# Block-sparse attention feeding a soft mixture of experts: k and q of a head pair transposed into one PSUM tile and copied out at once, loads issued at other places in a pair

## The chip, the cores and the metric

The kernel runs on one core of a Trainium2 chip. The metric is the device time of one execution in microseconds, as the median of several executions. "The profiled execution" is one further execution, recorded by the hardware profiler; its span goes from its first to its last recorded instruction.

The engines are named as in the profile: PE is TensorE's matrix multiplication and PEld its weight loads, DVE is VectorE, ACT is ScalarE, POOL is GpSimd, SP is SyncE. PSUM is the memory that TensorE writes to; here it has eight banks.

## What is computed

Attention over 4 batches × 8 heads, 768 positions, 64 dimensions a head, with keys in 24 chunks of 32. Each query keeps six chunks, chosen by an upper bound of its scores; then a soft mixture of experts over the 3072 × 512 result:

```python
k_min = np.min(k_chunks, axis=3); k_max = np.max(k_chunks, axis=3)
ub = sum_d(maximum(q * k_min, q * k_max))            # one bound per query and chunk
ub = np.where(causal, ub, -1e9)
top_chunks = np.argsort(ub, axis=-1)[..., -6:]
scores = scale * q @ k.T                             # kept where selected and causal
x = softmax(scores) @ v                              # 3072 x 512 after the heads are joined

logits = x @ phi                                     # 512 x 32: 8 experts of 4 slots
slot_input = softmax(logits, over tokens).T @ x
slot_out[e] = relu(slot_input[e] @ w1[e]) @ w2[e]    # w1 512 x 1024, w2 1024 x 512
out = softmax(logits, over slots) @ slot_out         # 3072 x 512 f32
```

## The kernel before

**Tiling.** Two heads make a pair: 128 partitions hold 2 × 64 dimensions. There are 16 pairs, four to a batch. k and q arrive in bf16 with positions on the partitions, and TensorE transposes them, six column blocks of 128 positions for each of two heads. Scores are computed transposed, keys on partitions and queries in columns, and only the causal blocks, packed in six groups (`GROUPS`, L29). The prediction calls them s0 to s5 (`scores(i, g)`, L316) and their exponentials on ScalarE e0 to e5 (`expo(i, g)`, L340). Groups 0, 1 and 4 have 2 × 512 columns, groups 2, 3 and 5 have 2 × 384.

**Order.** The order of instructions on each engine is the order of the Python calls, written by hand (`tc.manual_schedule()`, L84). An engine works its list in order; a wait holds up all that stands behind it. Between engines the pools decide: a tile drawn from a pool takes the buffer of the tile drawn `bufs` earlier under the same tag, and its first writer waits for the last reader of that tile. The PSUM pools are (L88 to L90): `p_sc`, two buffers of two banks, tag "sc", for the score tiles; `p_at`, one buffer of two banks for the value product; `p_tp`, two buffers of one bank, tag "tp", for all transposes and bounds.

**One pair** `i` of the main loop (L618 to L696) works on five pairs at once. In the order of the calls:

- `scores`/`expo` groups 0 and 1 of pair i. `mask` (L353), called by `expo`, zeroes the blocks on the diagonal on GpSimd.
- `ubound(i+1)` (L272): thirteen matmuls of the split q (`qpn`) with the chunk minima and maxima (`bd`).
- `normalise(i-2)` (L380, DVE).
- `select(i+1)` (L289): twelve DVE maxima of eight, a cast on GpSimd (L296, "the selection's cast"), one comparison on DVE.
- `transposes(i+2, "k")` (L225) into a "tp" tile, `evac_T(i+2, "k")` (L237): a ScalarE copy to `kT`.
- `load(i+5)` (L147) of k and q: DMA issues from GpSimd, f32 to bf16 on the way, into a ring of five.
- `pv(i-1)` (L362), the value product, blocks 0 to 2; score groups 2 and 3; `x_transposes(i-2)` (L393); `pv` block 3.
- `transposes(i+2, "q")` and `evac_T(i+2, "q")`; `kmin` (L246), `evac_x` (L405), `kmax` (L252) on DVE.
- `load_v(i+2)` (L160) and `weights(i)` (L555): DMA issues from GpSimd. `wplan` (L552) says how many of the experts' 16 weights of 1 MB each pair issues; `load_w` (L137) issues first the eight of w1, then the eight of w2 in the order `LATE` (L79), so that the last one issued is that of expert 4.
- score groups 4 and 5; `ns_transposes(i+1)` (L302) and `evac_ns(i+1)` (L311, DVE), which bring the selection to the form in which the scores add it; `pv` blocks 4 and 5; `qsplit(i+2)` (L262, DVE).

The selection enters a score group as extra matmuls (L333) that accumulate a large negative number from `nsT`.

The pairs 3, 7 and 11 are each the last of a batch; the mixture's softmax for the batch runs three pairs later, in pairs 6, 10 and 14 (`slots`, L619; the calls `moe(...)`), its logits two pairs later, in pairs 5, 9 and 13. In the slots pairs the k and q loads stand behind score group 3. Pairs 0 to 2 are transposed in the prologue (L561 to L616).

**After the loop** (from L698): the last pair's values, the last batch's logits and softmax, `experts_in` (L824, uses w1), `experts_out` and `shared_out` (L864, L872, w2), `last_expert_out` (L888, the last weight loaded), then the product with the slots' outputs, scaled and stored in 512 KB pieces.

Of the kernel before, what the change touches and what calls it, by code (L numbers as in the profile page):

```python
# [10 lines left out]
BF16 = mybir.dt.bfloat16  # L11
# [48 lines left out]
def kernel(  # L60
# [10 lines left out]
    nc = tc.nc  # L71
# [9 lines left out]
    EARLY = 14  # L81
# [13 lines left out]
    ident = static.tile([P, P], BF16, name="ident")  # L95
# [29 lines left out]
    tp3 = i_ctx.enter_context(tc.tile_pool(name="tp3", bufs=3, side="right"))  # L125
# [11 lines left out]
    def load_w(i):  # L137

        if i < E:
            src = moe_w1[i].rearrange("(a p x) f -> p a (x f)", p=P, x=2)  # L140
            dst = w_sb[i].rearrange("p (a f) -> p a f", a=NDG // 2)
        else:
            src = moe_w2[LATE[i - E]].rearrange("(a p x) d -> p a (x d)", p=P, x=4)
            dst = w_sb[i].rearrange("p (a f) -> p a f", a=NFG // 4)
        nc.gpsimd.dma_start(out=dst, in_=src)  # L145

    def load(i, nm):  # L147

        b, j = divmod(i, NPB)
        t = ring[nm][i % 5]  # L150
        src = {"k": k, "q": q}[nm][b, 2 * j:2 * j + 2]
        nc.gpsimd.dma_start(out=t, in_=src.rearrange("h (p g) d -> p h (g d)", p=P))  # L152
        st[nm, i] = t
# [6 lines left out]
    def load_v(i):  # L160
        b, j = divmod(i, NPB)
        nc.gpsimd.dma_start(  # L162
            out=v_t[i % NV][:, :, :, :D],
            in_=v[b, 2 * j:2 * j + 2].rearrange("h (g p) d -> p h g d", p=P),
        )
# [59 lines left out]
    def transposes(i, nm):  # L225

        ps = p_tp.tile([P, NQT, P], BF16, name="tr_ps", tag="tp")
        src = st.pop((nm, i))
        for g in range(NQT):
            for h in range(2):  # L230
                nc.tensor.matmul(  # L231
                    ps[h * 64:(h + 1) * 64, g, :], lhsT=src[:, h, g * D:(g + 1) * D], rhs=ident,
                    is_transpose=True,
                )
        st[nm + "ps", i] = ps

    def evac_T(i, nm):  # L237

        t = tp3.tile([P, S], BF16, name=nm + "T", tag=nm + "T")
        nc.scalar.copy(  # L240
            t.rearrange("d (p g) -> d p g", g=NQT),
            st.pop((nm + "ps", i)).rearrange("d g p -> d p g"),
        )
        st[nm + "T", i] = t

    def kmin(i):  # L246
        kT = st["kT", i].rearrange("d (c x) -> d c x", x=CH)
# [24 lines left out]
    def ubound(i):  # L272
        ps = p_tp.tile([P, NJ, 2, 2, NCHUNK], F32, name="ub_ps", tag="tp")
        qpn, bd = st.pop(("qpn", i)), st.pop(("bd", i))
        nc.tensor.matmul(
            ps.rearrange("p j h x c -> p (j h x c)"), lhsT=qgrp.rearrange("p a b -> p (a b)"),
            rhs=caus.rearrange("p j h x c -> p (j h x c)"), start=True, stop=False,
        )
        for t in range(NQT):
            o = ps[:, t % NJ, :, t // NJ, :]  # L280
            for x in range(2):
                nc.tensor.matmul(  # L282
                    o, lhsT=qpn[:, x, t * P:(t + 1) * P],
                    rhs=bd[:, x],
                    start=False, stop=(t == NQT - 1 and x == 1),
                )
        st["ubps", i] = ps
# [28 lines left out]
    def scores(i, g):  # L316
        ps = p_sc.tile([P, 2, 512], F32, name="sc_ps", tag="sc")
        kT, qT, nsT = st["kT", i], st["qT", i], st["nsT", i]
        for kg, q0, w, c in (GROUPS_LAST if i == LAST else GROUPS)[g]:
            qs = slice(kg * P + q0, kg * P + q0 + w)  # L320
            for h in range(2):
                r = slice(h * 64, (h + 1) * 64)
                nc.tensor.matmul(  # L323
                    ps[:, h, c:c + w], lhsT=kT[r, kg * P:(kg + 1) * P], rhs=qT[r, qs],
                    start=True, stop=False,
                )
            t0, t1 = kg + q0 // P, kg + (q0 + w) // P
            runs = [(x, max(t0, x * NJ), min(t1, (x + 1) * NJ)) for x in range(2)]
            runs = [r for r in runs if r[1] < r[2]]
            for x, f, l in runs:  # L330
                for h in range(2):
                    r = slice(h * 64, (h + 1) * 64)
                    nc.tensor.matmul(  # L333
                        ps[:, h, c + (f - t0) * P:c + (l - t0) * P],
                        lhsT=smask[r, x, kg].rearrange("p a b -> p (a b)"),
                        rhs=nsT[r, (f - x * NJ) * P:(l - x * NJ) * P], start=False, stop=(l == t1),
                    )
        st["scps", i, g] = ps

    def expo(i, g, masked=True):  # L340
        pieces = (GROUPS_LAST if i == LAST else GROUPS)[g]
        w = sum(x[2] for x in pieces)
        if w == 512:
            e = ep.tile([P, 2, 512], BF16, name="e_sb", tag="e_sb")
        else:
            e = ep3.tile([P, 2, 384], BF16, name="e3_sb", tag="e3_sb")
        nc.scalar.activation(e[:, :, :w], st.pop(("scps", i, g))[:, :, :w], func=ACT.Exp, scale=scale)  # L347

        st["e", i, g] = e
        if masked:  # L350
            mask(i, g)
# [191 lines left out]
    def have(i):  # L543
        return 0 <= i < NPAIR

    def moe(step, i):

        if have(i) and i % NPB == NPB - 1:
            step(i // NPB)


    wplan = {1: 1, 3: 1, 4: 1, 5: 1, 7: 1, 8: 1, 9: 1, 10: 1, 11: 1, 12: 1, 13: 2, 14: 1, 15: 1}  # L552
    nw = 2

    def weights(i):  # L555
        nonlocal nw
        for _ in range(wplan.get(i, 0)):
            load_w(nw)
            nw += 1
# [58 lines left out]
    for i in range(1, NPAIR):  # L618
        slots = have(i - 3) and (i - 3) % NPB == NPB - 1  # L619
        if i >= EARLY:  # L620
            wt = ctx.enter_context(tc.tile_pool(name=f"wt{i}", bufs=1))
            w_sb.append(wt.tile([P, NFG * Dm], BF16, name=f"w_sb{i}"))
            weights(i)
        scores(i, 0)
        expo(i, 0)
        moe(moe_max, i - 3)
        scores(i, 1)
        expo(i, 1)
        if have(i + 1):
            ubound(i + 1)  # L630
        moe(moe_bound, i - 3)
        if have(i - 2):
            normalise(i - 2)
        if i == LAST:
            moe_ct_copy(B - 2)
        if have(i + 1):
            select(i + 1)
        moe(moe_comb, i - 3)
        if have(i + 2):
            transposes(i + 2, "k")  # L640
            evac_T(i + 2, "k")
        if have(i + 5) and not slots:
            load(i + 5, "k")
            load(i + 5, "q")
        pv(i - 1, [0, 1, 2])
        for g in (2, 3):
            scores(i, g)
            expo(i, g, not slots)
        moe(moe_exp, i - 3)
        if slots:  # L650
            mask(i, 2)
            mask(i, 3)
        if have(i + 5) and slots:
            load(i + 5, "k")
            load(i + 5, "q")
        if have(i - 2):
            x_transposes(i - 2)
        pv(i - 1, [3] if i < LAST else [3, 4])
        if have(i + 2):
            transposes(i + 2, "q")  # L660
            evac_T(i + 2, "q")
            kmin(i + 2)
        moe(moe_exp2, i - 3)
        if have(i - 2):
            evac_x(i - 2)
        if have(i + 2):
            kmax(i + 2)
        moe(moe_scale, i - 3)
        if have(i + 2):
            load_v(i + 2)  # L670
        if i < EARLY:
            weights(i)
        scores(i, 4)
        expo(i, 4)
        if i == LAST:
            pv(i - 1, [5])
        moe(moe_comb2, i - 3)
        scores(i, 5)
        expo(i, 5)
        if have(i + 1):  # L680
            ns_transposes(i + 1)
            evac_ns(i + 1)
        if i < LAST:
            pv(i - 1, [4])
        moe(moe_dispatch, i - 3)
        if i < LAST:
            pv(i - 1, [5])
        if have(i + 2):
            qsplit(i + 2)
        moe(moe_ct, i - 3)  # L690
        moe(moe_logits, i - 2)
        moe(moe_copy, i - 2)
        if i == LAST - 2:
            l_ctx.close()
        if i == LAST - 1:
            u_ctx.close()  # L696
# [71 lines left out]
    def cinv(n):  # L768
# [5 lines left out]
        lg2, lhsT=mneg.broadcast_to([NS, P]), rhs=rep.broadcast_to([NS, NQT, NS]),  # L774
# [4 lines left out]
        bc, lhsT=mneg.broadcast_to([NS, P]), rhs=identf[:NS, :NS], start=True, stop=True,  # L779
# [166 lines left out]
    for m in range(1, NM):  # L946
        o_sb = op.tile([P, 2, Dm], F32, name="o_sb", tag="o_sb")
        for x, scaled in enumerate((scaled_act, scaled_dve)):
            tag = ("sc", "tp", "tp", "sc", "at")[n % 5]
# [40 lines left out]
```

## Time and profile before

| | |
|---|---|
| median of 3 runs | 160.82 us (160.73 to 161.08) |
| profiled execution | 160.93 us |
| its span | 159.2 us |
| mean granted TensorE clock | 0.98 |
| moved by DMA | 32.92 MB, most of it from GpSimd's queue |
| pair loop, first exponential of pair 1 to that of pair 14 | 19.56 to 111.13 us |
| last weight: issued, landed | 117.84, 138.34 us |

The profile is a page of counts and groups made from the records of one execution, and the trace behind it can be asked for single instructions. A row of the timeline gives start, length, engine, source line and operation, the tiles written and read, their shapes, and how many instructions were put together in the row. A row of a grouped view gives the count, then the busy time and the mean length of one in nanoseconds, then the engine's idle time before them and what ended it. A row of the table by stretches gives for each engine its busy time and, in brackets, its instructions. Busy shares are in the first lines of the page; the two lines that run over 40 slices cut the span into equal parts of 3.98 us. For a DMA the page gives the median time from issue to landing.

### The profile page before, as it was taken

What the parts mean: (1) busy time and instruction counts of PE and PEld (TensorE: products, weight loads), DVE (VectorE), ACT (ScalarE), POOL (GpSimd) and SP (SyncE); (2) the same over time, 40 slices, a digit from 0 to 9 for tenths busy, and PEclk for the clock granted to TensorE, in tenths of its full rate; (3) what the DMA queues carried; (4) which work ended last, traced back from release to release, by engine and by line L of the source; (5) the groups of instructions that cost most, each with busy time, mean ns of one, the idle gap of its engine ahead of it and who ended that gap; (6) DMA issues with size and microseconds to landing.
All of it is one profiled execution on the core that took longest, in us unless ns stands there. A gap on an engine that the chain in (4) does not pass through costs nothing.

```text
span 159.2 us, 5923 instructions
## 1 busy us (share of the span) xinstructions
PE 138.0 (87%) x2436; PEld 93.5 (59%) x2436; DVE 123.5 (78%) x436; ACT 122.3 (77%) x168; POOL 102.3 (64%) x201
## 2 busy tenths in 40 slices
PE   7896789999999998999989989999898999978400
PEld 5473466767767676766767766767667854433000
DVE  5378889999999999999999699988952751287620
ACT  3378899999999898999978889998788632076510
POOL 6989779869889686989876957658774710000000
PEclk9999999999999999999999999999999999999965
DMA  3999999999999999999999999999999999239996
GB/s 40 157 172 203 187 206 208 185 203 203 184 208 198 203 204 201 203 185 205 200 204 202 201 206 202 199 206 196 207 206 215 216 213 207 54 118 406 405 402 250
DMA packets 40571, 32.92 MB, mean 207 GB/s; under 512 B 26336, under 2 KB 34784, under 8 KB 40544
## 3 DMA queue, kind: packets, MB, share of 16 engines
q0 software_dynamic: 38384, 26.25, 110.7%
q1 hardware_dynamic: 2160, 6.29, 10.1%
q8 instruction: 19, 0.31, 0.7%
q14 instruction: 8, 0.07, 0.1%
HBM read 52.49 MB, written 6.29 MB: 369 GB/s over the span
## 4 chain that ended last, share of the span: by engine, by line
DVE 39%; PE 30%; ACT 9%; DMA 8%; POOL 6%; issue 4%; DVEq 0%; POOLq 0%; SPq 0%; ACTq 0%
DVE mx L294 7%; DMA out_dram<-o_sb 5%; DVE x_sb L388 5%; ACT e_sb L347 5%; DVE mm L255 4%; DVE mm L249 4%; PE sc_ps L323 4%; PE at_ps L375 4%; DVE qpn L269 4%; PE sc_ps L333 3%; DMA q_in<-in_q_dram 3%; DVE ns_t L297 3%; DVE qpn L265 3%; PE h_ps L828 2%; PE xT_ps L397 2%
## 5 line engine op out<-in xcount | busy, mean ns | idle before, releaser
L347 ACT ACTIVATE e_sb<-sc_ps 128x1024 bf16<-128x1024 f32 (+1 forms) x96 | 83.3, 917 | 7.3 <-PE sc_ps L333 6.8
L357 POOL TENSOR_SCALAR_AFFINE_SELECT e_sb<-e_sb 128x256 bf16<-128x256 bf16 x96 | 38.3, 415 | 17.2 <-ACT e_sb L347 16.7
L323 PE MATMUL sc_ps<-qT,kT 64*128 64x384 bf16 (+3 forms) x258 | 36.8, 305 | 2.6 <-ACT e_sb L347 1.7
L333 PE MATMUL sc_ps<-nsT,smask 64*128 64x384 bf16 (+2 forms) x294 | 38.1, 284 | 0.1
L375 PE MATMUL at_ps<-v_t,e_sb 128*128 128x65 bf16 x642 | 28.4, 194 | 1.7 <-DVE x_sb L388 1.4
L375 PEld LDWEIGHTS <-e_sb 128*128 128x128 bf16 x642 | 24.5, 98 | 3.8 <-issue 2.5
L323 PEld LDWEIGHTS <-kT 64*128 64x128 bf16 x258 | 13.9, 93 | 10.7 <-issue 5.3
L294 DVE MAX8 mx<-ub_ps 128x8 f32<-128x8 f32 (+1 forms) x192 | 16.9, 164 | 2.9 <-PE ub_ps L282 2.6
L162 POOL DMA_DIRECT2D v_t<-in_v_dram x16 | 16.7, 1042 | 2.5 <-DMA w_sb<-in_moe_w_dram 1.5
L249 DVE TENSOR_REDUCE mm<-kT 128x24 bf16<-128x768 bf16 x16 | 15.1, 944 | 3.3 <-ACT kT L240 3.3
L333 PEld LDWEIGHTS <-smask 64*128 64x128 bf16 x294 | 14.9, 94 | 3.9 <-issue 0.6
L388 DVE TENSOR_TENSOR x_sb<-at_ps,inv 128x768 bf16<-128x768 f32 (+1 forms) x17 | 15.5, 911 | 0.6
L240 ACT COPY kT<-tr_ps 128x768 bf16<-128x768 bf16 x16 | 12.8, 801 | 3.9 <-PE tr_ps L231 3.9
L255 DVE TENSOR_REDUCE mm<-kT 128x24 bf16<-128x768 bf16 x16 | 15.1, 943 | 0.0
L240 ACT COPY qT<-tr_ps 128x768 bf16<-128x768 bf16 x16 | 12.8, 800 | 2.3 <-PE tr_ps L231 2.3
L145 POOL DMA_DIRECT2D w_sb<-in_moe_w_dram x16 | 11.4, 715 | 0.0
L152 POOL DMA_DIRECT2D k_in<-in_k_dram x14 | 10.3, 733 | 1.0 <-POOLq L974 0.8
L152 POOL DMA_DIRECT2D q_in<-in_q_dram x14 | 10.1, 718 | 0.1
L408 DVE COPY xT_sb<-xT_ps 128x768 bf16<-128x768 bf16 (+1 forms) x15 | 8.1, 537 | 2.5 <-PE xT_ps L397 2.5
L269 DVE TENSOR_SCALAR qpn<-qT 128x768 bf16<-128x768 bf16 x15 | 9.8, 651 | 0.0
L231 PE MATMUL tr_ps<-ident,k_in 128*64 128x128 bf16 x192 | 8.7, 229 | 0.5 <-DMA k_in<-in_k_dram 0.4
L231 PE MATMUL tr_ps<-ident,q_in 128*64 128x128 bf16 x192 | 8.4, 223 | 0.4 <-DMA q_in<-in_q_dram 0.2
(147 smaller groups left out, 208.8 us busy)
## 6 DMA issues: line engine op xcount, KB each, us to landing
w_sb<-in_moe_w_dram POOLq DMA_DIRECT2D x16, 1024.0 KB, 13.8
out_dram<-o_sb SPq DMA_DIRECT2D x10, 512.0 KB, 4.6
v_t<-in_v_dram POOLq DMA_DIRECT2D x16, 192.0 KB, 10.3
k_in<-in_k_dram POOLq DMA_DIRECT2D x14, 192.0 KB, 9.9
q_in<-in_q_dram POOLq DMA_DIRECT2D x14, 192.0 KB, 10.3
out_dram<-o_sb SPq DMA_DIRECT2D x2, 256.0 KB, 4.1
k_in<-in_k_dram POOLq DMA_DIRECT2D x1, 384.0 KB, 7.5
q_in<-in_q_dram POOLq DMA_DIRECT2D x1, 384.0 KB, 8.7
```

The costliest lines, as they stand in the source:

```text
L152: nc.gpsimd.dma_start(out=t, in_=src.rearrange("h (p g) d -> p h (g d)", p=P))
L231: nc.tensor.matmul(ps[h * 64:(h + 1) * 64, g, :], lhsT=src[:, h, g * D:(g + 1) * D], rhs=ident, is_transpose=True,)
L240: nc.scalar.copy(t.rearrange("d (p g) -> d p g", g=NQT), st.pop((nm + "ps", i)).rearrange("d g p -> d p g"),)
L249: nc.vector.tensor_reduce(mm[:, 0, 0, :], kT, axis=AX.X, op=ALU.min)
L255: nc.vector.tensor_reduce(mm[:, 1, 0, :], kT, axis=AX.X, op=ALU.max)
L294: nc.vector.max(mx[:, a, :], ub[:, a, :max(8, 4 * t + 4)])
L323: nc.tensor.matmul(ps[:, h, c:c + w], lhsT=kT[r, kg * P:(kg + 1) * P], rhs=qT[r, qs], start=True, stop=False,)
L333: nc.tensor.matmul(ps[:, h, c + (f - t0) * P:c + (l - t0) * P], lhsT=smask[r, x, kg].rearrange("p a b -> p (a b)"), rhs=nsT[r, (f - x * NJ ...
L347: nc.scalar.activation(e[:, :, :w], st.pop(("scps", i, g))[:, :, :w], func=ACT.Exp, scale=scale)
L357: nc.gpsimd.affine_select(out=e[:, :, c:c + P], in_=e[:, :, c:c + P], compare_op=ALU.is_ge, fill=0.0, base=0, pattern=[[0, 2], [1, P]], ch ...
L375: nc.tensor.matmul(o, lhsT=st["e", i, g][:, h, c:c + P], rhs=v_t[i % NV][:, h, kg, :], start=(kg == 0), stop=(kg == t),)
L388: nc.vector.tensor_tensor(st["x", b][:, t0:t1, 2 * j:2 * j + 2, :].rearrange("p t h d -> p h t d"), at[:, :, :, :D], inv.broadcast_to([P, ...
```

## The change

The changed kernel has three edits.

1. In the main loop the twelve transposes of k and the twelve of q are made together, between score groups 0 and 1 (`transposes_kq`). Their PSUM tile is drawn from the score pool, tag "sc", instead of two tiles from "tp". One ScalarE copy takes both out, into one tile `kqT` whose halves are `kT` and `qT`. Between transposes and copy nothing stands. The prologue keeps separate transposes and copies, into halves of the same kind of tile.
2. The k and q loads of pair i+5 are issued first in a pair, ahead of score group 0. The v load and the weights are issued behind `select(i+1)`, whose last GpSimd instruction is the cast, instead of behind `kmax`. In the slots pairs the k, q, v and weight loads stay where they were.
3. `wplan` issues no weight in pair 1, and two in pair 12 instead of one.

The places of `kmin`, `kmax`, `evac_x`, `qsplit` and of all else on DVE are unchanged.

```diff
+    def kq_tile(i):
+        t = tp3.tile([P, 2, S], BF16, name="kqT", tag="kqT")
+        st["kT", i], st["qT", i] = t[:, 0], t[:, 1]
+        return t
+
     def evac_T(i, nm):
 
-        t = tp3.tile([P, S], BF16, name=nm + "T", tag=nm + "T")
+        if nm == "k":
+            kq_tile(i)
         nc.scalar.copy(
-            t.rearrange("d (p g) -> d p g", g=NQT),
+            st[nm + "T", i].rearrange("d (p g) -> d p g", g=NQT),
             st.pop((nm + "ps", i)).rearrange("d g p -> d p g"),
         )
-        st[nm + "T", i] = t
+
+    def transposes_kq(i):
+
+        ps = p_sc.tile([P, 2, 1024], BF16, name="tr_ps", tag="sc")
+        for x, nm in enumerate(("k", "q")):
+            src = st.pop((nm, i))
+            for g in range(NQT):
+                for h in range(2):
+                    nc.tensor.matmul(
+                        ps[h * 64:(h + 1) * 64, x, g * P:(g + 1) * P],
+                        lhsT=src[:, h, g * D:(g + 1) * D], rhs=ident, is_transpose=True,
+                    )
+        nc.scalar.copy(
+            kq_tile(i).rearrange("d x (p g) -> d x p g", g=NQT),
+            ps[:, :, :S].rearrange("d x (g p) -> d x p g", g=NQT),
+        )
...
-    wplan = {1: 1, 3: 1, 4: 1, 5: 1, 7: 1, 8: 1, 9: 1, 10: 1, 11: 1, 12: 1, 13: 2, 14: 1, 15: 1}
+    wplan = {3: 1, 4: 1, 5: 1, 7: 1, 8: 1, 9: 1, 10: 1, 11: 1, 12: 2, 13: 2, 14: 1, 15: 1}
...
+        if have(i + 5) and not slots:
+            load(i + 5, "k")
+            load(i + 5, "q")
         scores(i, 0)
         expo(i, 0)
         moe(moe_max, i - 3)
+        if have(i + 2):
+            transposes_kq(i + 2)
         scores(i, 1)
         expo(i, 1)
...
         if have(i + 1):
             select(i + 1)
         moe(moe_comb, i - 3)
-        if have(i + 2):
-            transposes(i + 2, "k")
-            evac_T(i + 2, "k")
-        if have(i + 5) and not slots:
-            load(i + 5, "k")
-            load(i + 5, "q")
+        if not slots:
+            if have(i + 2):
+                load_v(i + 2)
+            if i < EARLY:
+                weights(i)
         pv(i - 1, [0, 1, 2])
...
         pv(i - 1, [3] if i < LAST else [3, 4])
         if have(i + 2):
-            transposes(i + 2, "q")
-            evac_T(i + 2, "q")
             kmin(i + 2)
...
         moe(moe_scale, i - 3)
-        if have(i + 2):
-            load_v(i + 2)
-        if i < EARLY:
-            weights(i)
+        if slots:
+            if have(i + 2):
+                load_v(i + 2)
+            if i < EARLY:
+                weights(i)
         scores(i, 4)
```

## The prediction, made before the changed kernel was run

> **What bounds the kernel now.** I read the page first, then the stretches between the first exponentials of successive pairs, then ScalarE's and TensorE's timelines of one plain pair.
>
> ```profile
> span 159.2 us, 5923 instructions
> PE 138.0 (87%) x2436; PEld 93.5 (59%) x2436; DVE 123.5 (78%) x436; ACT 122.3 (77%) x168; POOL 102.3 (64%) x201
> GB/s 40 157 172 203 187 206 208 185 203 203 184 208 198 203 204 201 203 185 205 200 204 202 201 206 202 199 206 196 207 206 215 216 213 207 54 118 406 405 402 250
> ```
>
> No engine stands out, and the loads run at about 200 GB/s from the second slice to the 34th. So I cut the pair loop at the start of each pair's first exponential. Columns: stretch, length, busy time of PE, PEld, DVE, ACT, POOL with instructions, clock, DMA share, GB/s.
>
> ```profile
> 19.56:26.46 6.90, 6.28 (x113) 4.09 (x109) 6.16 (x24) 6.58 (x10) 5.50 (x10) 1.00 1.32 208
> 26.46:32.96 6.50, 6.41 (x122) 4.52 (x122) 6.18 (x22) 6.46 (x9) 5.99 (x13) 1.00 1.57 185
> 53.03:61.35 8.32, 8.18 (x162) 6.13 (x164) 7.71 (x29) 7.45 (x13) 6.13 (x13) 1.00 1.35 201
> 61.35:68.03 6.68, 6.25 (x122) 4.38 (x116) 6.58 (x24) 6.46 (x8) 5.11 (x10) 1.00 1.21 207
> 81.62:90.50 8.88, 8.17 (x162) 6.12 (x164) 7.47 (x30) 7.64 (x13) 6.68 (x14) 1.00 1.34 203
> 90.50:97.57 7.07, 6.41 (x122) 4.47 (x117) 6.97 (x25) 6.47 (x9) 5.16 (x12) 1.00 1.29 201
> 104.07:111.13 7.06, 7.00 (x147) 5.13 (x146) 6.17 (x23) 6.48 (x10) 4.94 (x10) 1.00 1.37 202
> ```
>
> These are pairs 1, 2, 6, 7, 10, 11 and 13. From 19.56 to 111.13 there are 13 pairs in 91.57 us. Pairs 5 and 9 carry the same logits as 13, so 7.06 each; then 32.5 us are left for pairs 3, 4, 8, 12 and pair 2, 6.50 each. In a plain pair PE, DVE and ACT are all busy for 6.2 to 6.5 of 6.50 us: three loops of nearly one length, and whatever lengthens a link between them lengthens the pair. The granted clock is 1.00 throughout.
>
> ScalarE around pair 8 (start, length, instruction), and its two sizes of exponential grouped by shape:
>
> ```profile
> 67.22 1.83 ACT L347 ACTIVATE e_sb<-sc_ps 128x768 bf16<-128x768 f32 x2
> 68.03 1.94 ACT L347 ACTIVATE e_sb<-sc_ps 128x1024 bf16<-128x1024 f32 x2
> 69.86 0.81 ACT L240 COPY kT<-tr_ps 128x768 bf16<-128x768 bf16 x1
> 70.72 1.51 ACT L347 ACTIVATE e_sb<-sc_ps 128x768 bf16<-128x768 f32 x2
> 72.14 0.80 ACT L240 COPY qT<-tr_ps 128x768 bf16<-128x768 bf16 x1
> 74.56 1.94 ACT L347 ACTIVATE e_sb<-sc_ps 128x1024 bf16<-128x1024 f32 x2
> L347 ACT ACTIVATE e_sb<-sc_ps 128x1024 bf16<-128x1024 f32 x21 | 20.9, 1023 | 1.8 <-PE sc_ps L333 1.8
> L347 ACT ACTIVATE e_sb<-sc_ps 128x768 bf16<-128x768 f32 x22 | 17.1, 810 | 1.2 <-PE sc_ps L333 1.0
> ```
>
> Call a pair's exponentials e0 to e5 and its scores s0 to s5. The row at 67.22 is e5 of the pair before and e0 merged; e0 starts at 68.03, e1 0.92 later. Records of neighbours overlap by 0.10.
>
> TensorE in the same pair:
>
> ```profile
> 68.09 0.23 PE L323 MATMUL sc_ps<-qT,kT 64*128 64x128 bf16 x2
> ...
> 68.77 0.46 PE L282 MATMUL ub_ps<-bd,qpn 128*128 128x48 bf16 x12
> 69.16 0.53 PE L231 MATMUL tr_ps<-ident,k_in 128*64 128x128 bf16 x12
> 69.65 0.54 PE L375 MATMUL at_ps<-v_t,e_sb 128*128 128x65 bf16 x12
> ...
> 70.46 0.33 PE L323 MATMUL sc_ps<-qT,kT 64*128 64x384 bf16 x2
> ...
> 70.88 0.51 PE L397 MATMUL xT_ps<-ident,x_sb 128*128 128x128 bf16 x6
> 71.23 0.41 PE L375 MATMUL at_ps<-v_t,e_sb 128*128 128x65 bf16 x8
> 71.57 0.53 PE L231 MATMUL tr_ps<-ident,q_in 128*64 128x128 bf16 x12
> 72.03 0.28 PE L323 MATMUL sc_ps<-qT,kT 64*128 64x256 bf16 x2
> ...
> 72.48 0.33 PE L323 MATMUL sc_ps<-qT,kT 64*128 64x384 bf16 x2
> ...
> 72.90 0.34 PE L305 MATMUL ns_ps<-ident,ns_t 128*128 128x128 bf16 x3
> 73.08 0.86 PE L375 MATMUL at_ps<-v_t,e_sb 128*128 128x65 bf16 x22
> 73.92 0.39 PE L323 MATMUL sc_ps<-qT,kT 64*128 64x512 bf16 x2
> 74.13 0.40 PE L333 MATMUL sc_ps<-nsT,smask 64*128 64x128 bf16 x4
> ```
>
> The reader is to see two things. The score tiles have two buffers: s1 starts at 68.09, 0.06 after the end of e5 (67.22 + 0.81 = 68.03), whose buffer it takes; it does not wait for e0. And the two ScalarE copies stand where they cover TensorE: kT's beside the bound, the first values and s2, qT's (72.14) beside s4.
>
> At the other end, the last weight's first use, and the end of the load stream:
>
> ```profile
> 138.68 0.39 PE L893 MATMUL so_last<-w_sb,hT_pad 128*32 128x256 bf16 x8
> 138.00:139.00 1.00, 1.00 (x24) 0.52 (x17) 0.10 (x1) 0.00 (x0) 0.00 (x0) 1.00 0.06 16
> ```
>
> Bytes still land after 138.0 and the expert that needs them starts at 138.68. So a shorter pair loop is worth 0.7 us at most, while a longer one is paid in full.
>
> **The change part by part.** *Transposes and copies.* Two groups of 12 transposes, two copies of about 0.70 net (0.80 less the 0.10 overlap) go; one group of 24 and one copy of 1536 columns come. TensorE's work is the same: 69.16 to 69.65 and 71.57 to 72.03 are 0.95 together, as 24 in a row at most that, at least 0.8 without the gap behind each. The copy's price is not in the trace. From below: the two exponential shapes differ by 1023 - 810 = 213 ns for 256 columns, 0.83 ns each, so 768 more columns than 0.70 make 1.33. From above: twice the record, 1.60. I take 1.33, since the shapes on the same engine scale so; work saved on ScalarE: 0.07 a pair, and up to 0.16 of idle behind kT's copy.
>
> But the new tile is drawn from the score tiles' two buffers, between s0 and s1. The ring becomes s0, kq, s1, s2 ..., so kq takes the buffer of e5, s1 must wait for e0, and s2 for the copy. TensorE runs in order: behind the waiting s1 stand the bound of the next pair (VectorE's selection waits for it), the values of the pair before, and s2. Two chains then close on themselves.
>
> Chain one, from e0's start: e0 0.92, copy 1.33, e1 1.02 with its tail, 0.06 to release: s3 starts at 3.33. Then by the starts above: s3 to xT 0.42, xT 0.35, values 0.34, (q's transposes are gone), s4 0.45, s5 0.42, ns 0.18, values 0.84, s0 until the next e0 0.64 (73.92 to 74.56). Sum 6.97. The transposes kq start when e5 is released, about 0.1 before e0's start, and end 0.9 after: just in time for the copy at 0.92.
>
> Chain two goes through VectorE:
>
> ```profile
> 69.47 1.05 DVE L294 MAX8 mx<-ub_ps 128x8 f32<-128x8 f32 x12
> 73.40 0.35 DVE L313 COPY nsT<-ns_ps 128x384 bf16<-128x384 bf16 x1
> 104.97 0.30 PE ub_ps L282 x12
> 105.37 1.06 DVE L294 MAX8 mx<-ub_ps 128x8 f32<-128x8 f32 x12 [0.49 <-PE ub_ps L282]
> ```
>
> e0 1.02, release 0.06, s1 to the bound's matmuls 0.68 (68.09 to 68.77), 0.40 from these to the first maximum (104.97 to 105.37, a place where VectorE did wait), 4.28 from the maxima to the end of nsT's copy (69.47 to 73.75), 0.06, then 0.43 from the masked part of s0 to e0 (74.13 to 74.56). Sum 6.93. VectorE, without a gap today, gets about 0.5 us of idle in front of the maxima, so how long the q split takes beside GpSimd no longer counts.
>
> So a plain pair takes 6.97 for 6.50: +0.47, five times, 2.35. Pairs 5, 9 and 13 add the logits ahead of s0, worth 7.06 - 6.50 = 0.56 on top: 7.53, +0.47 three times, 1.41. Pair 7: 6.97 for 6.68, +0.29. Pair 11 (7.07) and pair 1 (6.90, without x's transposes in its chain) +0. In pairs 6 and 10, 0.8 of transposes go ahead of s1 and 0.95 away behind it; s3 comes a copy later, s4 about half a microsecond, of which ScalarE's extra exponentials and PE's idle (8.17 of 8.88 in pair 10) hide a part: +0.4 and +0.3, between 0 and 0.8. Pairs 14 and 15 have no kq. Total 4.75.
>
> By the Trainium skill (page Perfetto Trace Analysis, section Optimizing Scalar/DVE Operations), grouping into larger operations improves throughput if the engine is saturated, while breaking them up may let work end sooner where the engine only causes bubbles on others. ScalarE at 6.46 of 6.50 looks like the first case, whose result is the rival below; by its second sentence the sum stays as above.
>
> *Loads.* k and q (two issues) go to the front of GpSimd's pair, ahead of its masks, v and the weight ahead of the masks of groups 2 to 4, behind the selection's cast. GpSimd has the same 5.99 us of work per pair, now in 6.97; the masks of group 4, last in the pair, are wanted only by the first values, about 2.2 us into the next pair. Cost 0. One megabyte leaves pair 1 and comes back in pair 12.
>
> ```profile
> v_t<-in_v_dram POOLq DMA_DIRECT2D x16, 192.0 KB, 10.3
> POOL v_t L162 <- DMA w_sb<-in_moe_w_dram: 1.5, 1, 1.5
> ```
>
> At 207 GB/s that is 5 us less queue for the pairs between, and v still has 10.3 - 5 = 5.3 us from issue to landing: the stream hardly runs dry, cost 0. If it does, the last weight lands later by the gap; 0.7 covers it today, 4.75 more then. The second row shows an issue held until an earlier load had landed; with q moved forward in pair 2 this may come again, behind it that pair's masks and cast, which are wanted late: 0 to 1.5, taken 0.
>
> **The sum.** The profiled execution took 160.93 for its span of 159.2, 0.11 over the median of the runs, 160.82. 160.93 + 4.75 = 165.7.
>
> **The rivals.** *Heavier:* the copy, over two banks, costs 1.60. Chain one becomes 7.24, in the ten pairs that it sets +0.27: 168.4. Against it stands the even slope of the exponentials.
>
> *Lighter:* s1's wait is partly absorbed, because transposes no longer stand between the later scores, and the pair settles halfway at 6.75: 163.4. The sums of two chains so near each other speak against it.
>
> *Not slower:* ScalarE is the loop that counts, the merged copy gives it 0.07 to 0.23 a pair, 0.9 to 3 us in 13, and the last weight lets 0.3 of it through, 0.7 at most: 160.6 with the former. For it: ScalarE has hardly any idle in a plain pair. Against it: s1's wait for e0 stands in the changed kernel's instruction order. It decides only if a pair stays under 6.50. This is also the case in which the skill's grouping rule holds.
>
> *Dry loads:* the pairs stay at 6.50, and the stream breaks off in the middle for the 5 us taken from its queue; the last expert then waits 5 - 0.7: 165.1, for another reason. The 5.3 us left speak against it.
>
> **How the numbers follow.** Forecast 0.62 (165.7), heavier 0.20, lighter 0.09, not slower 0.07, dry loads 0.02. The range takes the first three: from the lighter case, 163.4, to a little above the heavier one, 168.8. About 0.2% is what a measurement of this kernel can tell from no change. Of the 0.07, 0.04 is faster and 0.03 no change: slower 0.93.
>
> **What would show it.** Right: s1 starts about 0.06 after e0's end in pairs 2 to 13; VectorE waits some 0.5 us for the bound before its maxima; the copy takes about 1.43 as a record; ScalarE idles before e4; a plain pair takes 6.97. Wrong: plain pairs of 6.50 or less; a copy near 1.6; GpSimd holding the first values; the last expert waiting for its weight.

## The result, and the profile after

The changed kernel takes 171.17 us (median of 6 runs, 171.01 to 171.66) beside 160.95 for the kernel before (6 runs): ratio 1.0612, 95% interval 1.0578 to 1.0646. It is slower, as forecast, but by 10.2 us where 4.75 were forecast, and outside the range.

The head of the page of the changed kernel, and three of its groups (count, busy time, mean length in ns, then the idle time before them and what ended it):

```profile
span 169.4 us, 5911 instructions
PE 138.2 (82%) x2435; PEld 92.5 (55%) x2436; DVE 125.1 (74%) x436; ACT 121.6 (72%) x155; POOL 101.6 (60%) x201
...
L315 DVE MAX8 mx<-ub_ps 128x8 f32<-128x8 f32 (+1 forms) x192 | 16.9, 162 | 11.9 <-PE ub_ps L303 11.9
...
L262 ACT COPY kqT<-tr_ps 128x1536 bf16<-128x1536 bf16 x13 | 18.7, 1435 | 0.7 <-PE tr_ps L258 0.7
...
L278 DVE TENSOR_TENSOR bd<-mm,headsel 128x96 bf16<-128x96 bf16 x16 | 8.8, 547 | 0.5
```

The first of the three in the kernel before:

```profile
L294 DVE MAX8 mx<-ub_ps 128x8 f32<-128x8 f32 (+1 forms) x192 | 16.9, 164 | 2.9 <-PE ub_ps L282 2.6
```

The busy times differ by under 2 us from those before: most of the 10 us are waits. The merged copy takes 1.435 as a record, as forecast, and VectorE now waits 11.9 us for the bound, 2.6 before. The third row was not among the costliest before: the multiplication that spreads the chunk minima and maxima over the heads (`bd`, called by `kmax`) has a mean of 547 ns.

Four stretches from one pair's first exponential to the next (pairs 2, 3, 13 and 14; columns as in the prediction):

```profile
26.52:33.62 7.10, 6.47 (x126) 4.45 (x126) 5.82 (x23) 6.42 (x8) 5.93 (x13) 1.00 1.60 185
33.62:41.63 8.01, 6.50 (x126) 4.45 (x126) 6.98 (x23) 6.41 (x7) 6.52 (x14) 1.00 1.62 171
...
113.06:120.60 7.54, 6.87 (x146) 4.94 (x144) 7.00 (x24) 6.41 (x7) 5.61 (x12) 1.00 1.29 206
120.60:129.00 8.40, 7.29 (x134) 5.28 (x136) 6.34 (x28) 6.24 (x12) 6.30 (x15) 1.00 1.27 205
```

Pairs 2 and 3 do the same work, and 3 is 0.9 longer; VectorE is busy for 1.16 more in it. Pair 14 has no merged transposes, and yet takes 8.40 for 7.65.

The same cut in most pairs (1 and 12 left out), for the kernels of this study (us; the names are those of the experiments below):

| | 2, 4 | 3 | 8 | 5 | 9, 13 | 7 | 11 | 6 | 10 | 14 |
|---|---|---|---|---|---|---|---|---|---|---|
| before | 6.50 | 6.51 | 6.53 | 7.06 | 7.06 | 6.69 | 7.06 | 8.32 | 8.88 | 7.65 |
| after | 7.09, 7.10 | 8.01 | 8.01 | 8.01 | 7.54 | 8.05 | 8.03 | 9.02 | 8.64 | 8.40 |
| merge_only | 7.10 | 7.11 | 7.10 | 7.54 | 7.54 | 7.10 | 7.42 | 9.36 | 9.20 | 8.39 |
| loads_only | 6.50 | 6.71 | 6.51 | 7.30 | 7.06 | 6.69 | 7.06 | 8.25 | 8.77 | 7.65 |
| bd_act | 7.17 | 7.17 | 7.16 | 7.54 | 7.54 | 7.17 | 7.43 | 8.93 | 8.63 | 8.40 |
| v_back | 7.09 | 7.10 | 7.10 | 7.54 | 7.54 | 7.10 | 7.41 | 9.05 | 8.98 | 8.40 |
| kq_back | 7.10, 7.35 | 7.10 | 7.10 | 7.54 | 7.54 | 7.10 | 8.05 | 8.79 | 8.96 | 8.41 |
| merge_later | 7.08 | 7.08 | 7.08 | 7.88 | 7.67 | 7.08 | 7.53 | 8.73 | 9.13 | 7.70 |
| max_later | 7.09 | 7.10 | 7.10 | 7.54 | 7.54 | 7.09 | 7.49 | 9.26 | 9.38 | 8.40 |
| bd_pool | 7.01, 6.95 | 6.95 | 6.95 | 8.08 | 7.54 | 7.39 | 8.26 | 8.40 | 8.44 | 8.11 |
| relu_act | 7.10 | 7.10 | 7.10 | 7.54 | 7.54 | 7.10 | 7.46 | 8.63 | 8.48 | 7.69 |

The first exponential of pair 1 stands at 19.56 in before and after, that of pair 15 at 118.78 and 129.00: all 10.2 us are in this loop.

ScalarE and TensorE of the changed kernel at the start of pair 3 (start, length, instruction, idle time before and what ended it):

```profile
33.62 1.02 ACT L368 ACTIVATE e_sb<-sc_ps 128x1024 bf16<-128x1024 f32 x1 [0.26 <-PE sc_ps L354]
34.54 1.43 ACT L262 COPY kqT<-tr_ps 128x1536 bf16<-128x1536 bf16 x1
35.86 2.45 ACT L368 ACTIVATE e_sb<-sc_ps 128x1024 bf16<-128x1024 f32 x3
38.73 1.73 ACT L368 ACTIVATE e_sb<-sc_ps 128x1024 bf16<-128x1024 f32 x2 [0.42 <-PE sc_ps L354]
```

```profile
34.69 0.23 PE L344 MATMUL sc_ps<-kqT 64*128 64x128 bf16 x2 [0.32 <-ACT e_sb L368]
...
35.37 0.46 PE L303 MATMUL ub_ps<-bd,qpn 128*128 128x48 bf16 x12
```

e0 ends at 34.64 and s1 starts at 34.69: it waits for e0, not for the e5 of the pair before. e1 starts 2.24 after e0 in place of 0.92, and ScalarE idles before e4. That is the forecast mechanism. What the forecast did not have is in VectorE and GpSimd of the same pair:

```profile
38.73 0.94 DVE L276 TENSOR_REDUCE mm<-kqT 128x24 bf16<-128x768 bf16 x1
39.70 1.17 DVE L278 TENSOR_TENSOR bd<-mm,headsel 128x96 bf16<-128x96 bf16 x1
40.80 0.34 DVE L334 COPY nsT<-ns_ps 128x384 bf16<-128x384 bf16 x1
```

```profile
37.33 0.23 POOL L317 CAST ns_t<-mx 128x12 bf16<-128x12 f32 x1
37.55 1.03 POOL L162 DMA_DIRECT2D v_t<-in_v_dram  x1
38.57 0.70 POOL L145 DMA_DIRECT2D w_sb<-in_moe_w_dram  x1
39.27 1.49 POOL L378 TENSOR_SCALAR_AFFINE_SELECT e_sb<-e_sb 128x256 bf16<-128x256 bf16 x4
40.73 0.71 POOL L152 DMA_DIRECT2D k_in<-in_k_dram  x1
```

And the same two engines in pair 3 of the kernel before:

```profile
37.05 0.94 DVE L255 TENSOR_REDUCE mm<-kT 128x24 bf16<-128x768 bf16 x1
38.03 0.26 DVE L257 TENSOR_TENSOR bd<-mm,headsel 128x96 bf16<-128x96 bf16 x1
```

```profile
37.07 0.77 POOL L357 TENSOR_SCALAR_AFFINE_SELECT e_sb<-e_sb 128x256 bf16<-128x256 bf16 x2
37.79 1.03 POOL L162 DMA_DIRECT2D v_t<-in_v_dram  x1
38.82 0.71 POOL L145 DMA_DIRECT2D w_sb<-in_moe_w_dram  x1
```

Before, two masks were done by the time bd came, and GpSimd was issuing v's load while bd took 0.26. After, the two issues come first, the masks wait behind them and then run four in a row, and bd, which starts 0.06 after one of them, takes 1.17: it ends at 40.87, 0.11 after the last mask (39.27 + 1.49 = 40.76). nsT's copy stands behind bd, the masked part of the next s0 behind that, and e0 behind this. Much the same happens in the pairs 5, 7, 8 and 11. Pairs 4 and 9 escape narrowly: there bd starts 0.18 and 0.12 before the first of the masks and takes 0.26.

### The profile page after: what moved, and what is told of

It is laid out like the page before. It is cut to its first block, busy times and chain, and to the rows that moved or that the text cites. A ratio compares the mean times of both kernels' runs of the same rounds, so it can differ in the third digit from the quotient of the medians.

```text
span 169.4 us, 5911 instructions
## 1 busy us (share of the span) xinstructions
PE 138.2 (82%) x2435; PEld 92.5 (55%) x2436; DVE 125.1 (74%) x436; ACT 121.6 (72%) x155; POOL 101.6 (60%) x201
## 4 chain that ended last, share of the span: by engine, by line
PE 34%; DVE 27%; DMA 14%; ACT 12%; POOL 5%; issue 4%; DVEq 0%; POOLq 0%; ACTq 0%; SPq 0%
ACT e_sb L368 9%; DMA v_t<-in_v_dram 7%; PE sc_ps L344 6%; PE sc_ps L354 5%; DMA out_dram<-o_sb 5%; DVE mx L315 5%; PE at_ps L396 4%; DVE bd L278 4%; DVE mm L276 4%; DVE mm L270 4%; DMA k_in<-in_k_dram 3%; PE h_ps L852 2%; PE xT_ps L418 2%; DVE xT_sb L429 2%; PE ub_ps L303 2%
## 5 line engine op out<-in xcount | busy, mean ns | idle before, releaser
L378 POOL TENSOR_SCALAR_AFFINE_SELECT e_sb<-e_sb 128x256 bf16<-128x256 bf16 x96 | 38.8, 427 | 28.9 <-ACT e_sb L368 28.6
L344 PE MATMUL sc_ps<-kqT 64*128 64x384 bf16 (+3 forms) x258 | 37.0, 306 | 9.4 <-ACT e_sb L368 9.2
L354 PE MATMUL sc_ps<-nsT,smask 64*128 64x384 bf16 (+2 forms) x294 | 38.7, 284 | 3.6 <-DVE nsT L334 3.4
L315 DVE MAX8 mx<-ub_ps 128x8 f32<-128x8 f32 (+1 forms) x192 | 16.9, 162 | 11.9 <-PE ub_ps L303 11.9
L344 PEld LDWEIGHTS <-kqT 64*128 64x128 bf16 x258 | 15.0, 93 | 18.9 <-issue 13.2
L262 ACT COPY kqT<-tr_ps 128x1536 bf16<-128x1536 bf16 x13 | 18.7, 1435 | 0.7 <-PE tr_ps L258 0.7
L270 DVE TENSOR_REDUCE mm<-kqT 128x24 bf16<-128x768 bf16 x16 | 15.1, 944 | 3.2 <-ACT kqT L246 3.2
L276 DVE TENSOR_REDUCE mm<-kqT 128x24 bf16<-128x768 bf16 x16 | 15.1, 943 | 0.0
L152 POOL DMA_DIRECT2D k_in<-in_k_dram x14 | 10.2, 727 | 1.5 <-POOLq L998 0.8
L278 DVE TENSOR_TENSOR bd<-mm,headsel 128x96 bf16<-128x96 bf16 x16 | 8.8, 547 | 0.5
L246 ACT COPY kqT<-tr_ps 128x768 bf16<-128x768 bf16 x6 | 4.8, 795 | 5.6 <-PE tr_ps L231 5.6
L418 PE MATMUL xT_ps<-ident,x_sb 128*128 128x128 bf16 x96 | 8.3, 221 | 0.3 <-DVE x_sb L409 0.3
L975 PE MATMUL o_ps<-so_all,cT_all 128*128 128x512 bf16 x21 | 6.3, 377 | 1.8 <-ACT o_sb L937 1.4
```

What stands on the lines that cost most here:

```text
L262: nc.scalar.copy(kq_tile(i).rearrange("d x (p g) -> d x p g", g=NQT), ps[:, :, :S].rearrange("d x (g p) -> d x p g", g=NQT),)
L270: nc.vector.tensor_reduce(mm[:, 0, 0, :], kT, axis=AX.X, op=ALU.min)
L276: nc.vector.tensor_reduce(mm[:, 1, 0, :], kT, axis=AX.X, op=ALU.max)
L278: nc.vector.tensor_tensor(bd, mm.broadcast_to([P, 2, 2, NCHUNK]), headsel.broadcast_to([P, 2, 2, NCHUNK]), op=ALU.mult,)
L315: nc.vector.max(mx[:, a, :], ub[:, a, :max(8, 4 * t + 4)])
L344: nc.tensor.matmul(ps[:, h, c:c + w], lhsT=kT[r, kg * P:(kg + 1) * P], rhs=qT[r, qs], start=True, stop=False,)
```

## The experiments

**Which edit costs what.** merge_only is edit 1 alone: the changed kernel with the loads and the plan of weights as before.

```diff
-    wplan = {3: 1, 4: 1, 5: 1, 7: 1, 8: 1, 9: 1, 10: 1, 11: 1, 12: 2, 13: 2, 14: 1, 15: 1}
+    wplan = {1: 1, 3: 1, 4: 1, 5: 1, 7: 1, 8: 1, 9: 1, 10: 1, 11: 1, 12: 1, 13: 2, 14: 1, 15: 1}
...
-        if have(i + 5) and not slots:
-            load(i + 5, "k")
-            load(i + 5, "q")
         scores(i, 0)
...
         moe(moe_comb, i - 3)
-        if not slots:
-            if have(i + 2):
-                load_v(i + 2)
-            if i < EARLY:
-                weights(i)
+        if have(i + 5) and not slots:
+            load(i + 5, "k")
+            load(i + 5, "q")
...
         moe(moe_scale, i - 3)
-        if slots:
-            if have(i + 2):
-                load_v(i + 2)
-            if i < EARLY:
-                weights(i)
+        if have(i + 2):
+            load_v(i + 2)
+        if i < EARLY:
+            weights(i)
```

> Edit 1 alone: k and q in one tile from the score ring, one copy; loads and weights issued where they were before. Theory A (two causes): the merged tile between s0 and s1 makes a plain pair 7.0 to 7.1 us, as in the pairs 2, 4 and 12 of the changed kernel, and the moved issues cost the rest, by pushing the masks to where VectorE's bd multiplication comes. Then bd takes 0.26 to 0.35 us in every pair, no pair but 6 and 10 is 8 us long, and the time is 171.2 - 5 x 0.92 (pairs 3, 5, 7, 8, 11) - 0.75 (pair 14) = 165.8, between 165 and 167. Rival B (the merged copy is the whole cost, the issues none): 170 to 171.5, with the 8.0 us pairs still there.

Measured: 168.11 us, ratio 1.0418 (1.0365 to 1.0472). No plain pair is near 8 us any more, and bd takes 0.26 in all pairs of the loop but 1 (0.35) and 6 (0.44), as A has it. But the time is 2.3 above A's 165.8: pair 14 keeps its 8.39, and pairs 6 and 10 are longer still than in the changed kernel. So edit 1 costs 7.0 (168.11 for 161.09 of before in the same runs), and the edits 2 and 3 add 3.1 on top of it.

loads_only is edits 2 and 3 alone, on the kernel before; its diff is those hunks of the change.

> Edits 2 and 3 alone: transposes and copies as before, the loads and weights issued at the new places and by the new plan. Theory A: the masks of groups 2 to 4 stand behind the issues, run in a row when bd comes, and hold it in several pairs; since VectorE has no gap in a plain pair of before, each costs up to 0.9: 162.5 to 166, bd near 1.17 in the pairs that became longer. Rival C (the load stream runs dry): bd stays at 0.26 and the longer pairs wait for a landing. If the issues cost nothing without the merged copy: 160.9, within 0.5.

Measured: 162.08 for 161.09, ratio 1.0050 (1.0019 to 1.0080). Its group of bd, by smallest, median and largest length in ns:

```profile
L257 DVE TENSOR_TENSOR bd<-mm,headsel x16: 257/259/486, 8.5 to 109.5; 128x96 bf16<-128x96 bf16 x16
```

bd is held in the same five pairs (3, 5, 7, 8, 11), but for 0.48, not 1.17: it comes 0.06 after the last mask of a run has begun, where in the changed kernel two more follow. Only pairs 3 and 5 get visibly longer, by 0.2 each, and the loop of the profiled execution by 0.35 in all. So A's place was right and its price too high: the time lies below its range. More of the 1.0 stands at the other end, in the view of the last expert's tile:

```profile
  DMA w_sb<-in_moe_w_dram: 0.6, 1
```

The last weight is issued 0.37 later than before (118.21 for 117.84) and lands 1.45 later (139.79 for 138.34), and the last expert waits 0.6 for it. So part of the load stream does come late here, though not for the pairs, as C had it. Which of the edits 2 and 3 delays the weight was not taken apart. The two groups of edits cost more together (10.2) than apart (7.0 and 1.0).

**Is it bd, or data that come late?** In bd_act the changed kernel makes bd on ScalarE, two small copies behind e5:

```diff
+        for h in range(2):
+            nc.scalar.activation(
+                bd[:, :, h, :], mm[:, :, 0, :], func=ACT.Copy, scale=headf[:, h:h + 1])
```

> The changed kernel, with the bd multiplication taken from VectorE and made as two small ScalarE copies with a scale behind e5; loads where the change puts them. Theory A (VectorE's bd is held by the masks): the pairs 3, 7, 8 and 11 come down from 8.0 to 7.0 to 7.2, pair 5 to 7.5 to 7.7, the time to 171.2 - 4.6 = 166.6, between 165.5 and 167.5. Rival C (these pairs wait for late data): within 0.5 of 171.2.

Measured: 168.22, ratio 1.0433 (1.0374 to 1.0491): pairs 3, 7, 8 and 11 come down by 0.6 to 0.9, and the 3 us of the moved loads are gone with the loads still moved. It is bd, not the stream. The time itself lies above what A gave, since pair 5 fell by 0.47 only (the logits' pair has 7.54 for another reason), and since the copies now lengthen a plain pair to 7.17:

```profile
40.18 0.56 ACT L278 ACTIVATE bd<-mm,headf 128x48 bf16<-128x48 bf16 x2
40.63 1.02 ACT L380 ACTIVATE e_sb<-sc_ps 128x1024 bf16<-128x1024 f32 x1
```

They stand right in front of the next e0. One thing more is seen here: in the pairs 3, 5, 7 and 8 the masks now hold the first half of the q split, for 1.14 to 1.17, and these pairs are no longer than the others of their kind. The split stands behind nsT's copy. So in these pairs the cost is not that VectorE is held, but that it is held ahead of nsT's copy.

**Which of the moved issues?** v_back is the changed kernel with v and weights behind `kmax` again; its diff is the last two hunks of merge_only's, without the lines on k and q. kq_back is the counterpart, with the hunks on k and q alone.

v_back:

> The changed kernel with v and weights issued behind kmax again, as before; k and q loads first in a pair and the new plan of weights stay. Theory A (v and weights behind the cast push the masks of groups 2 to 4 under bd): bd is 0.26 us in every pair, no plain pair is longer than 7.2, and the time is that of edit 1 alone, 168.1, within 0.6. Rival D (k and q at the front, or the plan, do it): some pairs stay at 8.0 and the time at 170 to 171.5.

Measured: 167.80, ratio 1.0430 (1.0402 to 1.0458), plain pairs as with edit 1 alone. That is A, but for one bd of 0.44 in pair 6, beside the issue of a load. Its bd:

```profile
L278 DVE TENSOR_TENSOR bd<-mm,headsel x16: 257/258/441, 8.6 to 115.8; 128x96 bf16<-128x96 bf16 x16
```

kq_back:

> The changed kernel with the k and q loads behind the selection again; v and weights stay behind the cast, the plan of weights stays new. Theory A (v and weights alone push the masks under bd): bd still takes over 0.9 in at least two pairs, and pairs of 8.0 remain. Rival D (only k and q at the front bring the pair to that): bd 0.26 everywhere, near 168.

Measured: 168.08 in a single run. Neither theory as it stood: bd takes 0.93 in pair 11 (8.05), 0.51 and 0.46 in pairs 4 and 9, 0.44 in pair 6, and 0.26 in the others. Pair 11 has no k and q left to load, so its GpSimd list is that of the changed kernel. In pairs 4 and 9 no mask runs beside bd; the issue of the weight begins 0.2 after its start. In pair 3 all four issues now stand ahead of the masks, which start at 40.44, after bd:

```profile
37.25 0.72 POOL L152 DMA_DIRECT2D k_in<-in_k_dram  x1
37.97 0.72 POOL L152 DMA_DIRECT2D q_in<-in_q_dram  x1
38.67 1.04 POOL L162 DMA_DIRECT2D v_t<-in_v_dram  x1
39.69 0.74 POOL L145 DMA_DIRECT2D w_sb<-in_moe_w_dram  x1
40.44 2.03 POOL L378 TENSOR_SCALAR_AFFINE_SELECT e_sb<-e_sb 128x256 bf16<-128x256 bf16 x5
```

So, where k and q are still loaded, it takes both moves: v and the weight push the masks back by 1.7, which is just far enough to run when bd comes; with k and q issued there as well, the masks come after bd.

**Which chain sets 7.10 in a plain pair?** bd_pool: edit 1 alone, bd of the main loop on GpSimd.

```diff
-        nc.vector.tensor_tensor(
+        nc.gpsimd.tensor_tensor(
             bd, mm.broadcast_to([P, 2, 2, NCHUNK]), headsel.broadcast_to([P, 2, 2, NCHUNK]), op=ALU.mult,
```

> Edit 1 alone, with the bd multiplication of the main loop on GpSimd at the same place of the program instead of VectorE. Theory G (a plain pair of 7.10 is set by VectorE's chain, from the maxima over bd to nsT's copy, and the chain over the copy and the exponentials follows at 6.97): taking 0.26 from VectorE makes plain pairs 6.95 to 7.0, not 6.84, and the time 167.0 to 167.7. Rival H (the chain over the copy sets 7.10 as it is): plain pairs stay at 7.10, 168.1 within 0.4. Should GpSimd's multiplication come late for the next bound, 168.5 or more.

Measured: 167.73, ratio 1.0423 (1.0373 to 1.0473). Pair 3 of this kernel:

```profile
33.60:40.55 6.95, 6.32 (x125) 4.48 (x125) 5.65 (x22) 6.41 (x7) 5.20 (x12) 1.00 1.22 205
```

6.95 and not 6.84: with VectorE's chain 0.26 shorter, the chain over the copy takes over where the forecast had put it (6.97). That is G by the pairs; the time alone, at the edge of both ranges, does not tell G from H. The starts agree. In pair 3 of merge_only the masked part of s0 starts 0.06 after the end of nsT's copy (40.13):

```profile
39.78 0.35 DVE L334 COPY nsT<-ns_ps 128x384 bf16<-128x384 bf16 x1
40.19 0.39 PE L354 MATMUL sc_ps<-nsT,smask 64*128 64x128 bf16 x4
```

In bd_pool it starts 0.21 after it (39.92, 40.13), so there it waits for something else. The total gains little, since pairs 5, 7 and 11 became longer. That was not taken apart.

**Does the place between s0 and s1 matter?** merge_later: edit 1 alone, with the merged transposes and copy behind the selection.

```diff
         moe(moe_max, i - 3)
-        if have(i + 2):
-            transposes_kq(i + 2)
         scores(i, 1)
...
         moe(moe_comb, i - 3)
+        if have(i + 2):
+            transposes_kq(i + 2)
```

> Edit 1 alone at another place: the merged transposes and copy stand behind the selection, where k's stood before, so that the ring is s0, s1, kq, s2; loads and weights as before. Theory A1 (the place between s0 and s1 costs, since s1 and the bound behind it wait for e0): s1 starts before e0 ends, a plain pair is 6.5 to 6.7 and the time 160 to 163. Rival A2 (any third tile in a ring of two costs a full exponential, wherever it is drawn): plain pairs near 7.0, 165 to 167.

Measured: 168.44, ratio 1.0447 (1.0380 to 1.0514), plain pairs 7.08: A2 in the plain pairs, while the time lies above the ranges of both. s1 starts right behind s0 as A1 expected (e1 0.92 after e0), but the wait moved. The chain that ended last, in pair 3:

```profile
36.79 0.87 PE tr_ps L258 x24
...
37.69 1.45 ACT kqT L262
...
39.18 0.34 PE sc_ps L344 x2
```

TensorE transposes for 0.87, ScalarE copies for 1.45, and only then may s3 take the tile's buffer; beside the copy TensorE has the first values and s2 alone. Nearly the same length comes from another cycle. In this ring of two, the merged tile makes a plain pair about 0.6 longer at either place that was tried.

**Why are pairs 6, 10 and 14 longer?** First idea, max_later: edit 1 alone, with the maximum moved.

```diff
         expo(i, 0)
-        moe(moe_max, i - 3)
...
         expo(i, 1)
+        moe(moe_max, i - 3)
         if have(i + 1):
```

> Edit 1 alone, with the mixture's maximum (moe_max, in pairs 6, 10 and 14) moved from behind e0 to behind e1. Theory E (in these pairs TensorE waits for VectorE at the transposition of the maximum, and s1, in 6 and 10 the merged transposes too, stand behind it): from e0 to e1 the time in pairs 6 and 10 comes from 3.2 down to 2.3 to 2.5, in pair 14 from 1.58 to 0.92, and the whole to 165.5 to 167. Rival F (VectorE is late in any case, and the wait comes back at the bound): within 0.6 of 168.1.

Measured: 169.21, ratio 1.0508 (1.0444 to 1.0573). e1 follows e0 by 2.24 in pairs 6 and 10 and by 0.92 in 14, nearly as E said, yet the pairs are within 0.2 of merge_only's (9.26, 9.38, 8.40). That speaks for F, though the time lies above its range. The wait that the trace named was not the one that counted. The chain of merge_only from pair 13 into 14, and that of the kernel before:

```profile
116.37 0.27 DVE nsT L334
116.64 0.54 DVE qpn L286
117.18 0.70 DVE qpn L290
117.88 0.27 DVE pm L450
...
118.20 0.30 PE pmT_ps L457
...
118.97 0.97 DVE x_sb L409
...
119.98 0.54 PE at_ps L396 x12
```

```profile
111.08 0.23 PE pmT_ps L436
...
111.79 0.97 DVE x_sb L388
```

Before, the maximum waited for TensorE, and the normalisation (x_sb) started 0.66 after e0 (111.13). With edit 1 VectorE arrives late: behind nsT's copy it still has two halves of the q split (0.62 and 0.78 beside GpSimd's issues, 0.40 and 0.34 before), and the normalisation starts 1.40 after e0 (117.57). The difference, 0.74, is what pair 14 lost.

Second idea, relu_act: edit 1 alone, the second half of the q split of the pairs 7, 11 and 15, made in 5, 9 and 13, on ScalarE.

```diff
-        if i == 0:
+        if i == 0 or i in (7, 11, 15):
             nc.scalar.activation(t[:, 1, :], qT, func=ACT.Relu)
```

> Edit 1 alone, with the second half of the q split made on ScalarE (Relu, behind e5) instead of VectorE in the pairs 5, 9 and 13, which carry the logits. Theory J (in these pairs the q split and the mixture's maximum stand on VectorE behind nsT's copy, and the normalisation of the next pair, which the values wait for, behind them; 0.7 of the split less makes the pairs 6, 10 and 14 shorter): pair 14 from 8.39 to 7.6 to 7.8, pairs 6 and 10 each down by 0.4 to 0.8, the time to 165.8 to 167.2. Rival K (these pairs are long for their own work, whatever VectorE does before): within 0.5 of 168.1.

Measured: 166.02, ratio 1.0292 (1.0262 to 1.0322). Pair 14 takes 7.69, and pairs 6 and 10 0.7 less each; 2.1 us in all from three instructions moved. That is J.

**Versions of the kernel before.** before_variant has bd on GpSimd and `moe_max` behind e1, before_max_later the second alone; the diffs are those above. before_relu has one half of a q split (made in pair 9, `i in (0, 11)` in relu_act's line) on ScalarE.

before_variant:

> The kernel before with two moves only: bd on GpSimd, and moe_max behind e1. VectorE gets 0.26 a pair, TensorE no wait at the maximum in pairs 6 and 10. If the pair loop gets shorter, the last weight lets 0.7 us of it through: 160.2 to 160.9. If bd on GpSimd delays the loads or holds VectorE's q split longer: 161 to 162.

before_max_later:

> The kernel before with one move: moe_max from behind e0 to behind e1. TensorE's wait at the maximum in pair 10 (0.48 between e0 and e1 more than elsewhere) goes, 0.2 to 0.5 of it shortens the loop, and the last weight lets it through: 160.4 to 160.9. If the wait comes back at the bound, 161.0 within 0.3.

before_relu:

> The kernel before, with the second half of one q split (that made in pair 9) on ScalarE. In pair 10 of before s1 waits 0.48 for the mixture's maximum, behind two halves of 0.88 and 0.81 on VectorE; ScalarE is idle for 0.55 there and the half takes it about 0.7. If the wait goes and e0 comes 0.15 to 0.2 later, pair 9 and 10 together are 0.2 to 0.4 shorter and the time is 160.4 to 160.9 beside some 161.0 of before; if pair 10 is bound elsewhere, it is 161.0 to 161.2.

Measured: 163.64, ratio 1.0162 (1.0135 to 1.0188); 161.71, ratio 1.0034 (1.0007 to 1.0061); 161.08, ratio 0.9999 (0.9980 to 1.0018). The first two are slower than any of their forecasts. In the first, bd stands in GpSimd's list and the masks behind it come later; the chain of waits of its pair 5 runs over two of them (47.55) into the values (48.39). In the second, pairs 6 and 14 are longer by 0.32 and 0.44; why was not taken apart. The third falls in the range given for "pair 10 is bound elsewhere", but not for that reason: its loop is 0.7 shorter (98.5 between the first exponentials of pairs 1 and 15, for 99.2; pair 10 takes 8.27 for 8.88), and the time is the same. In the view of the last expert's tile:

```profile
L893 PE MATMUL so_last<-w_sb,hT_pad x8: 269/272/283, 138.9 to 139.1; 128*32 128x256 bf16 x8
...
  DMA w_sb<-in_moe_w_dram: 0.5, 1
```

The last expert now waits 0.5 for the last weight, which lands at 138.88, not earlier than before. No version here beats the kernel before.

## Why the prediction was wrong, step by step

The forecast is short by some 5.5 us. The loads, put at nothing, have 3.1 of them; pairs 6 and 14 have 1.4, the second chain 0.7, pair 11 has 0.4.

- **The cap by the last weight** was right, and before_relu shows it: a loop shorter by 0.7 gave nothing.
- **The ring** was right: in every pair with a merged tile ahead of s1, s1 starts 0.05 after the end of e0 or later. The copy's net price, 1.33, was right too (1.435 as a record, and e1 0.92 + 1.32 after e0). *Heavier* (1.60) and *lighter* (6.75) both fall; that edit 1 alone takes 168.11, beside the 168.4 of *heavier*, is chance.
- **Chain one**, 6.97, was right where it can be seen alone: 6.95 in bd_pool, and 7.54 for the forecast 7.53 in pairs 9 and 13, which stays in bd_pool too.
- **Chain two**, 6.93, was mis-sized, and it is the one that sets a plain pair. The term "0.40 from these to the first maximum" was a difference to a start in the view of waits (104.97), and it was added to a start in the timeline (68.77), which shows the same matmuls earlier (104.80 for 104.97). In one view, the timeline of pair 4 of merge_only, it is 0.57:

```profile
42.37 0.46 PE L303 MATMUL ub_ps<-bd,qpn 128*128 128x48 bf16 x12
...
42.94 1.06 DVE L315 MAX8 mx<-ub_ps 128x8 f32<-128x8 f32 x12 [0.38 <-PE ub_ps L303]
```

  With it chain two is 7.10, as measured. VectorE's idle ahead of the maxima is 0.38, not 0.5. Over pairs 2, 3, 4, 7, 8 and 12 this is 0.7 us.
- **The logits' and maximum's pairs.** "+0" for pair 14 was wrong (0.74), and "+0.4" for pair 6 too small (1.04 in merge_only). "+0.3" for pair 10 was met (0.32), but by luck: with three instructions off VectorE (relu_act) the pair is 0.40 shorter than in the kernel before. The sentence "how long the q split takes beside GpSimd no longer counts" is the step that failed here: it counts where the maximum and a normalisation stand behind the split. relu_act showed that. Pair 11's 0.36 was not taken apart. With these, the loop of merge_only is 7.1 longer (125.96 - 19.60 for 118.78 - 19.56) in place of 4.75.
- **Loads, "Cost 0"**, is the step that failed by most: 3.1 in the changed kernel. The prediction asked who waits for the masks, found only the first values, and did not ask which VectorE instruction runs while the masks do. It noted the split's slowing beside GpSimd and drew nothing from it for bd. bd held for 0.91 makes chain two 7.10 + 0.91 = 8.01, measured 8.01 in pairs 3, 5 and 8. Against edit 1 alone the five pairs lose 3.8 (0.90, 0.95, 0.91, 0.61 and, in pair 5, only 0.47), and 6 and 10 get back 0.9: ahead of them the split is shorter. Behind the held bd of pair 5 no GpSimd instruction runs beside it and it takes 0.34 and 0.34, for 0.68 and 0.79 in merge_only; in pair 9 it meets masks instead of issues and takes 0.35 and 0.56, for 0.67 and 0.80.
- **Dry loads** fell. Slices of the page within the loop go down to 114 GB/s, but the last weight lands at 147.47 and is first used at 148.90. Why the stream thins was not taken apart. In loads_only, where the loop is short, the last expert does wait, by 0.6.

By the Trainium skill (page SBUF — State Buffer, section SBUF: two separate sides), VectorE and GpSimd share a pair of ports; a VectorE instruction in a mode that uses both ports, or one with two inputs in SBUF beside a GpSimd instruction that reads SBUF, and the GpSimd instruction exclude each other, and whichever starts first keeps the pair for its whole instruction. The traces agree as to who is held: bd (two inputs in SBUF) and the q split vary, the reductions over chunks (one input) stay at 0.94 to 0.96 beside the same masks. As to how long, they show more than one instruction: one mask takes about 0.41, and bd was held through three of them, to 0.11 after the last.

## What to carry to other kernels

When an instruction is moved on one engine, list what runs at the new moment on an engine that it can hold (here VectorE beside GpSimd), and what stands behind that, not only who waits for its result; a price of nothing needs that list too. Add up starts from one view of the trace only, since two views can date the same instruction 0.17 us apart. And when two chains are within a tenth of each other, the tail behind the one that closes the loop (here two halves of a q split) can become late work for the next pair, even where the moved part itself is absent.

## What the runs showed of the hardware that was not expected

- A VectorE multiplication of 96 columns (bd), 0.26 alone, that began 0.03 to 0.07 after a mask on GpSimd was held, in nine cases of eleven, until the run of masks was over: 1.17 to 1.20 with three masks to go (pairs 3, 5, 7 and 8 of the changed kernel), 0.48 with one (loads_only, 0.49 in its pair 11). In each of these it ended 0.11 to 0.12 after the last mask. The other two are pair 11 of the changed kernel and of kq_back: with three to go bd took 0.93 and ended 0.26 before the last of them did. Where it began later in a mask, it ended 0.12 after that one, though another followed: 0.352 when it began 0.19 into it (pair 1 of before), 0.257 when it began 0.27 into it (pair 2 of the changed kernel). What decides between the two was not taken apart.
- A half of the q split takes 0.34 where it meets no GpSimd work; in most pairs of merge_only 0.67 to 0.80 beside the issuing of a v load and a weight. bd beside the issuing of v's load stayed at 0.26 (pair 3 of before), but took 0.44 where the issue of q's load began 0.11 before it (pair 6 of merge_only), and 0.51 and 0.46 where that of a weight began 0.2 after its start (pairs 4 and 9 of kq_back). In loads_only a half took 1.295 beside three masks.
- The same bd costs 0.35 on GpSimd, and two copies of 0.33 each (0.56 together) on ScalarE.
